# Chunked gated linear attention into a squared-ReLU FFN: all weight sums on VectorE, weight conversions closer together, attention pairs of the second group further apart

## The chip, the core and the metric

The kernel runs on one core of one Trainium2 chip. The metric is the device time of one execution in microseconds. Engines: TensorE (PE, with its weight loads PEld), VectorE (DVE), ScalarE (ACT), GpSimd (POOL), and SyncE (SP), whose queue issues all DMAs.

## What is computed

A gated linear recurrence over 768 tokens for 4 batches and 8 heads of width 48, and then a two-layer feed-forward network with squared ReLU over all 3072 tokens (model width 384, inner width 2048):

```python
for t in range(S):
    state = alpha[:, :, t, :, None] * state + np.einsum('bhd,bhe->bhde', k[:, :, t], v[:, :, t])
    y[:, :, t] = np.einsum('bhd,bhde->bhe', q[:, :, t], state)
...
h = np.maximum(x @ w_in, 0.0)
return (h * h @ w_out).astype(np.float32)
```

x is y with the heads side by side. The two weight matrices arrive as 64-bit floats; everything else is 32-bit.

## The kernel before

**Blocks and groups.** The tokens are cut into chunks of 128. Block n is chunk n//4 of batch n%4; there are 24 blocks. Four blocks (one chunk of every batch, 512 tokens) form a group; there are six. While the FFN of group g runs on TensorE, the attention of group g+1 is woven into it, in pairs of blocks.

**Attention of one block.** `ln` (logarithm of alpha, ACT), `cs` (cumulative sum as a product with a triangle, PE), `eb` and `ei` (exponentials, ACT), `mq` and `mk` (q and k scaled, L290, DVE), `turn` (transposes, L539, PE; PSUM tiles T), `kc` and `qc` (copies ks and qs, ACT). Then `ga` and `gb`: scores (L428) and sums for the state (L454) on PE, the mask `am` (L438) and the state's updates `us` and `s` (L465, L473, L474) on DVE, the products of y (L404) on PE, and `ev` (L562), which copies y into x on ACT. `ga` of a pair computes the scores of its first block and the first part of y of the pair before; `gb` does the scores of the second block and the rest of y.

The PSUM tiles of attention come in turn from one pool of four banks, `ps_att`: two for the transposes of each block, two for the scores of each block, two for the y of each pair, one for each `cs`. A tile can be written once the readers of the tile four places back are done. In the first group the scores of block 5 so take a bank that the scores of block 4 had (one `cs` lies between), and the scores of block 7 both banks of block 6 (with two of y between). The FFN has four banks of its own, `ps_ffn`.

**Conversion of the weights.** Each matrix comes in eight parts: w_in0 to 7 and w_out0 to 7, here also counted as index 0 to 15, 768 KB each in 64 bits, into four raw buffers. DVE takes exponent and upper mantissa out of the high words (L150, L154: `convert_first`), ACT turns the exponent and the low words (L163, L166: `convert_middle`), DVE puts them together (L172, L176, L179: `convert_second`). Indices 0 to 2 are started in a list written out by hand (`first`); the rest is spread over the first group by `next_weights`.

**FFN.** The first group multiplies plainly: units `ffn_in` j = 2 to 15 (L730, cost 2 each, 28 in all, with Relu and Square on ACT) and then 32 units `ffn_out` (L749, cost 1; part i of w_out is first used at unit 28 + 4i). The groups from the second on save products. The first layer (`layer_in`, L681, the order in the string `LAYER`) uses 20 sums of blocks of w_in (`W_SUMS`, `sum_w_in`) and 11 sums of blocks of x (`X_SUMS`, `sum_x`), all at L623. The second layer (`ffn_product`, L787) computes seven products for each four pairs of blocks in 28 units and needs sums of w_out: t1, t2, t3 (in place in w_out) and t4 for each of four r, 16 in all (`sum_w_out`). These sums are made once, the last ones during the second group.

**Who sets the order.** The program is recorded in one order, and each engine runs its instructions in that order. `weave` puts events between units: an event whose time is at most the sum of the costs so far is recorded ahead of the next unit. `attention` spreads the steps of a pair by the table `PLAN` (or `EARLY` in the first group), scaled: 2.35 in the first group, 1 later.

```python
events = [(4.0 * i, next_weights, ()) for i in range(2 * NW)]
```

At event i of these, load of index 4 + i, second half of index 2 + i, first half and middle of index 3 + i are recorded together.

Of the kernel before, what the change touches and what calls it, by code (L numbers as in the profile page):

```python
# [13 lines left out]
ALU = mybir.AluOpType  # L14
# [11 lines left out]
def kernel(  # L26
# [25 lines left out]
    nc = tc.nc  # L52
# [35 lines left out]
    NW = 8  # L88
# [3 lines left out]
    HM, NR2 = DM // 2, NJ // 4  # L92
# [29 lines left out]
    def load_weights(i):  # L122
        dst = (w_in + w_out)[i]
        dt = moe_w_in.dtype
        raw = dst if dt == FP32 else raw_pool.tile(list(dst.shape), dt, tag="raw", name="raw")
        raws[i] = raw
        if i < NW:
            src = moe_w_in[:, i * DF // NW : (i + 1) * DF // NW]
            nc.sync.dma_start(out=raw, in_=src.rearrange("(k r) f -> r k f", r=128))
        else:  # L130
            i -= NW
            src = moe_w_out[i * DF // NW : (i + 1) * DF // NW, :]
            nc.sync.dma_start(out=raw, in_=src.rearrange("(j r) m -> r j m", r=128))
# [6 lines left out]
    def convert_first(i):  # L140
        if moe_w_in.dtype == FP32:
            return
        w = (w_in + w_out)[i].rearrange("a k f -> a (k f)")
        n = w.shape[1]
        words = raws.pop(i).rearrange("a k f -> a (k f)").bitcast(U32)
        words = words.rearrange("a (n h) -> a n h", h=2)
        lo, hi = words[:, :, 0], words[:, :, 1]
        power = cv_pool.tile([128, n], U32, tag="power", name="power")
        upper = cv_pool.tile([128, n], U32, tag="upper", name="upper")
        nc.vector.tensor_scalar(  # L150
            out=power, in0=hi, scalar1=20, scalar2=0x7FF,
            op0=ALU.logical_shift_right, op1=ALU.bitwise_and,
        )
        nc.vector.tensor_scalar(  # L154
            out=upper, in0=hi, scalar1=0xFFFFF, scalar2=None, op0=ALU.bitwise_and
        )
        half[i] = w, lo, hi, power, upper

    def convert_middle(i):
        if moe_w_in.dtype == FP32:  # L160
            return
        w, lo, hi, power, upper = half[i]
        nc.scalar.activation(  # L163
            out=power, in_=power, func=AF.Relu, scale=2.0**23, bias=rebias
        )
        nc.scalar.activation(out=w, in_=lo, func=AF.Copy, scale=2.0**-52, bias=1.0)  # L166

    def convert_second(i):
        if moe_w_in.dtype == FP32:
            return  # L170
        w, lo, hi, power, upper = half.pop(i)
        nc.vector.scalar_tensor_tensor(  # L172
            out=power, in0=hi, scalar=0x80000000, in1=power,
            op0=ALU.bitwise_and, op1=ALU.bitwise_or,
        )
        nc.vector.scalar_tensor_tensor(  # L176
            out=w, in0=upper, scalar=2.0**-20, in1=w, op0=ALU.mult, op1=ALU.add
        )
        nc.vector.tensor_tensor(out=w, in0=w, in1=power.bitcast(FP32), op=ALU.mult)  # L179
# [1 line left out]
    for n, xs in ((0, "aqk"), (1, "aqk")):  # L181
        load(n, xs)
    to_load = list(range(2 * NW))
    stage = [3]

    def next_weights():
        i = stage[0]
        stage[0] += 1
        if to_load:
            load_weights(to_load.pop(0))  # L190
        if i <= 2 * NW:
            convert_second(i - 1)
        if i < 2 * NW:
            convert_first(i)
            convert_middle(i)


    NAM = 2
    am_t = kept("am", NAM, [128, 2, NP, 128])
# [418 lines left out]

    acc, ws, sums = {}, {}, {}

    def combine(steps, engine=nc.vector):
        for o, x, op, z in steps:
            engine.tensor_tensor(out=o, in0=x, in1=z, op=op)  # L623

    def parsed(text):
        for word in text.split():
            o, x, op, z = re.fullmatch(r"(\d+)=(\d+)([+-])(\d+)", word).groups()
            yield int(o), int(x), ALU.add if op == "+" else ALU.subtract, int(z)

    def w_slot(i):  # L630
        if i < 4 * KM:
            c, kk = divmod(i, KM)
            return w_in_t[:, 2 * c : 2 * c + 2, kk, :]
        r, i = divmod(i - 4 * KM, 3)
        if r not in ws:
            ws[r] = raw_pool.tile([128, 3, 2, 256], FP32, tag="raw", name="ws")
            if r == 2:
                sums.update({3: ws[r][:, 2]})
        return ws[r][:, i]
# [4 lines left out]

    w_sums = list(parsed(W_SUMS))

    def sum_w_in(i, engine):
        o, x, op, z = w_sums[i]
        combine(((w_slot(o), w_slot(x), op, w_slot(z)),), engine)

    def sum_x(g):
        if not xs_ready:
# [59 lines left out]
    def sum_w_out(i):  # L712
        i, r = divmod(i, NR2)
        t1, t2, t4 = (t[r] for t in tsum)
        b11, b12 = w_out[r][:, :, 0:HM], w_out[r][:, :, HM:DM]
        b21, b22 = w_out[NR2 + r][:, :, 0:HM], w_out[NR2 + r][:, :, HM:DM]
        o, x, z = ((t1, b12, b11), (t2, b22, t1), (b12, b22, b12), (t4, b21, t2))[i]
        combine(((o, x, ALU.subtract, z),), nc.gpsimd if i > 1 else nc.vector)

    def halves(j):  # L720
        return hid[j][:, :, 0:HT], hid[j][:, :, HT : 2 * HT]
# [49 lines left out]
    def ffn_product(g, i, r):  # L771
# [62 lines left out]
    steps = {f.__name__: f for stage in stages for f in stage}  # L834
# [12 lines left out]
        weights1 y0 cs3 ev0 br1 kT2 qT2 zeros2 ei3 kc2 qc2 kv1 eb3 mk3 load4v kT3 first0  # L847
        st0 mq3 weights2 load4q load4k middle0 sc2 kc3 qT3 second0 qc3 bl3 am2 br3 st1 br2
        kv2 sc3 am3 ha0 first1 ha1 middle1 y2 ev2 load4a hb0 first2 hb1 second1 st2 kv3
        middle2 st3 weights3  # L850
    """
    for word in first.split():
        f = max((x for x in steps if word.startswith(x)), key=len)
# [28 lines left out]
    def attention(pairs, scale):  # L882


        out = []
        for t, n0, after, *last in pairs:
            for at, fs in EARLY if n0 < SPLIT else PLAN:
                for f in fs.split():
                    w = t + at * scale
                    if f in ("ga", "gb"):  # L890
                        given = n0 - 2 if after else None, None if last or n0 >= NBLK else n0
                        out.append((w, {"ga": ga, "gb": gb}[f], given))
                    if last:
                        continue
                    if f == "ga" and n0 + 3 < NBLK:
                        out.append((w, load, (n0 + 3, "k")))
                    elif f == "gb":
                        for m, x in ((n0 + 2, "v"), (n0 + 3, "v"), (n0 + 4, "k")):
                            if m < NBLK:
                                out.append((w, load, (m, x)))  # L900
                    elif f == "turn":
                        if n0 < NBLK:
                            out.append((w, turn, (n0,)))
                            for m in range(n0 + 2, min(n0 + 4, NBLK)):
                                out.append((w, load, (m, "q")))
                    elif f != "ga" and n0 < NBLK:
                        n = n0 + int(f[-1])
                        out.append((w, steps[f[:-1]], (n,)))
                        if f[:-1] == "cs" and n + 2 < NBLK:
                            out.append((w, load, (n + 2, "a")))  # L910
        return sorted(out, key=lambda x: x[0])
# [13 lines left out]
    NG, NU = NBLK // GB, len(PRODUCTS) * NR2  # L925
    units = [(2, ffn_in, (0, j)) for j in range(2, NJ)]

    units += [(1, ffn_out, (0, t, i)) for i in range(NW) for t in range(GB)]
    events = [(4.0 * i, next_weights, ()) for i in range(2 * NW)]
    events += [(0, load, (GB + 1,)), (1.0, load, (GB + 2, "k"))]  # L930
    for i in range(len(w_sums)):
        at, engine = (44.1 + 0.5 * i, nc.gpsimd) if i < 9 else (51 + 0.2 * (i - 9), nc.vector)
        if i in (15, 16, 19):
            at, engine = 53.2, nc.gpsimd
        events.append((at, sum_w_in, (i, engine)))
    events += attention([(0, GB, False), (18.0, GB + 2, True), (27.5, GB + 4, True, True)], 2.35)
    events += [(54, sum_x, (1,))]
    weave(units, sorted(events, key=lambda x: x[0]))
    for g in range(1, NG):

        between = {}
        if g == 1:
            between = {3 + 5 * i: lambda i=i: sum_w_out(i) for i in range(4 * NR2)}
        layer_in(g, between)
        events = []
        if g + 1 < NG:
            n = GB * (g + 1) + 2
            pairs = [(0, n, True), (11.5, n + 2, True)]
            if g == 1:
                pairs = [(0, n - 2, False), (6.25, n, True), (12.5, n + 2, True)]  # L950
            events = attention(pairs, 1) + [(NU - 4.5, sum_x, (g + 1,))]
        weave([(1, ffn_product, (g, *u)) for u in PARTS], events)


# [28 lines left out]
```

## Time and profile before

| | us |
|---|---|
| median of three executions | 556.38 |
| lowest, highest | 553.46, 556.99 |
| profiled execution | 553.33 |
| span of its profile | 551.4 |

The page of the profile cuts the span into 40 slices of 13.8 us. A digit is the busy share in tenths; PEclk is the clock that TensorE was granted.

```profile
PE   8889999989999999999999999999999999999996
...
DVE  4988779599887773777673677664478651577530
ACT  4568875424264444236542327442326340326100
POOL 2010000562400000000000000000000000000000
PEclk9999999989999999999999999999999999999999
```

TensorE is the busy engine, except in the first three slices, in the ninth (110 to 124 us) and at the end. The first group lasts to 135.5 us, where L681 begins. GpSimd works in slices eight to twelve: these are the sums that the change moves. The costliest groups of instructions of those that the change concerns (busy in total, mean ns of one, then idle time of the engine ahead of them and what ended it):

```profile
L623 DVE TENSOR_TENSOR hid<-hid,h 128x512 f32<-128x512 f32 x130 | 88.4, 686 | 40.0 <-PE h L681 36.6
...
L749 PE MATMUL o<-w_out,hid 128*128 128x384 f32 x128 | 44.9, 505 | 2.9 <-DVE w_out L179 2.9
L730 PE MATMUL h<-x,w_in 128*128 128x512 f32 (+1 forms) x108 | 43.5, 551 | 3.3 <-ACT x L562 1.8
```

### The profile page before, as it was taken

How to read it: one execution, taken by the hardware profiler on the slowest of the kernel's cores; microseconds unless marked ns; L12 is line 12 of the kernel's file. 1: busy time of each engine (PE TensorE's matmuls, PEld its weight loads, DVE VectorE, ACT ScalarE, POOL GpSimd, SP SyncE). 2: the span in 40 equal slices, each digit the busy share in tenths (PEclk: the TensorE clock that was granted, in tenths of full speed). 3: DMA queues.
4: the chain of work that ended last, by engine and by line, in shares of the span. 5: the costliest groups of instructions: out<-in, count | busy, mean ns of one | idle time of the engine just before them, and what ended most of it. 6: DMA issues, size and time to landing. Idle time of an engine off the chain costs nothing.

```text
span 551.4 us, 12336 instructions
## 1 busy us (share of the span) xinstructions
PE 535.6 (97%) x5226; PEld 456.1 (83%) x5226; DVE 366.2 (66%) x636; ACT 236.0 (43%) x503; POOL 32.8 (6%) x46
## 2 busy tenths in 40 slices
PE   8889999989999999999999999999999999999996
PEld 5754456645889988988999988999988999988996
DVE  4988779599887773777673677664478651577530
ACT  4568875424264444236542327442326340326100
POOL 2010000562400000000000000000000000000000
PEclk9999999989999999999999999999999999999999
DMA  9977667511001654300342300153300000100001
GB/s 161 252 184 195 170 160 208 131 49 57 2 1 30 117 94 77 95 1 0 59 89 46 101 0 1 38 95 60 87 1 0 1 3 2 57 1 0 1 1 57
DMA packets 117086, 37.03 MB, mean 67 GB/s; under 512 B 108820, under 2 KB 111912, under 8 KB 117032
## 3 DMA queue, kind: packets, MB, share of 16 engines
q1 hardware_dynamic: 117032, 36.25, 28.9%
q8 instruction: 41, 0.67, 0.5%
q14 instruction: 13, 0.11, 0.1%
HBM read 31.49 MB, written 4.75 MB: 66 GB/s over the span
## 4 chain that ended last, share of the span: by engine, by line
PE 61%; DVE 2%; ACT 1%; issue 0%
PE o L787 29%; PE h L681 25%; PE y L404 3%; PE T L539 1%; PE sckv L428 1%; PE sckv L454 1%; ACT x L562 1%; PE cs L275 0%; DVE hid L623 0%; DVE am L438 0%; PE cs L274 0%; DVE us L812 0%; DVE hi L262 0%; DVE lo L263 0%; DVE s L473 0%
## 5 line engine op out<-in xcount | busy, mean ns | idle before, releaser
L623 DVE TENSOR_TENSOR hid<-hid,h 128x512 f32<-128x512 f32 x130 | 88.4, 686 | 40.0 <-PE h L681 36.6
L787 PE MATMUL o<-w_out,hid 128*128 128x192 f32 x480 | 82.6, 328 | 0.0
L787 PEld LDWEIGHTS o<-w_out,hid 128*128 128x128 f32 x480 | 78.5, 190 | 0.7
L681 PE MATMUL h<-xs,w_in 128*128 128x256 f32 x320 | 74.8, 379 | 0.0
L562 ACT COPY x<-y 32x256 f32<-32x256 f32 (+2 forms) x132 | 46.2, 364 | 55.5 <-PE y L404 52.1
L681 PEld LDWEIGHTS h<-xs,w_in 128*128 128x128 f32 x320 | 60.8, 190 | 8.1
L438 DVE COPY_PREDICATED am<-halves_mask,sckv 128x256 f32<-128x256 uint32 x40 | 15.6, 442 | 53.7 <-PE sckv L454 53.7
L681 PE MATMUL h<-x,ws 128*128 128x256 f32 x200 | 49.7, 380 | 0.0
L749 PE MATMUL o<-w_out,hid 128*128 128x384 f32 x128 | 44.9, 505 | 2.9 <-DVE w_out L179 2.9
L730 PE MATMUL h<-x,w_in 128*128 128x512 f32 (+1 forms) x108 | 43.5, 551 | 3.3 <-ACT x L562 1.8
L705 ACT COPY hid<-h 128x512 f32<-128x512 f32 x20 | 11.7, 585 | 78.0 <-PE h L681 78.0
L787 PE MATMUL o<-t,s 128*128 128x192 f32 x240 | 43.4, 328 | 0.0
L681 PEld LDWEIGHTS h<-x,ws 128*128 128x128 f32 x200 | 38.1, 190 | 5.1
L749 PEld LDWEIGHTS o<-w_out,hid 128*128 128x128 f32 x128 | 24.6, 197 | 20.5 <-DVE w_out L179 4.1
L681 PE MATMUL h<-x,w_in 128*128 128x256 f32 x160 | 40.3, 379 | 0.0
L787 PEld LDWEIGHTS o<-t,s 128*128 128x128 f32 x240 | 39.5, 190 | 0.3
L730 PEld LDWEIGHTS h<-x,w_in 128*128 128x128 f32 x108 | 20.1, 190 | 23.4 <-issue 16.2
L698 ACT ACTIVATE hid<-hid 128x512 f32<-128x512 f32 x55 | 34.7, 631 | 1.7
L681 PEld LDWEIGHTS h<-x,w_in 128*128 128x128 f32 x160 | 30.5, 190 | 4.1
L681 PE MATMUL h<-xs,ws 128*128 128x256 f32 x120 | 30.0, 380 | 0.0
L701 ACT ACTIVATE hid<-hid 128x512 f32<-128x512 f32 x35 | 22.0, 627 | 17.0 <-DVE hid L623 16.7
L787 PE MATMUL o<-t,hid 128*128 128x192 f32 x160 | 29.0, 332 | 0.0
(132 smaller groups left out, 786.8 us busy)
## 6 DMA issues: line engine op xcount, KB each, us to landing
raw<-in_moe_w_in_dram SPq DMA_DIRECT2D x8, 768.0 KB
raw<-in_moe_w_out_dram SPq DMA_DIRECT2D x8, 768.0 KB, 5.2
v_in<-in_v_dram SPq DMA_DIRECT2D x24, 192.0 KB, 4.4
out_dram<-osb SPq DMA_DIRECT2D x24, 192.0 KB, 2.0
k_in<-in_k_dram SPq DMA_DIRECT2D x23, 192.0 KB, 3.5
a_in<-in_alpha_dram SPq DMA_DIRECT2D x22, 192.0 KB, 2.6
q_in<-in_q_dram SPq DMA_DIRECT2D x22, 192.0 KB, 3.1
last<-row SPq DMA_DIRECT2D x40, 0.8 KB, 2.9
```

Of the source, the lines that this page charges most:

```text
L404: ins = nc.tensor.matmul(out=ys[e][64 * half : 64 * half + D + G * e, m % 2, p // 2, t], lhsT=lhsT, rhs=rhs, start=(half, e) not in seen, ...
L428: nc.tensor.matmul(out=ps[e][HALF[h], 0, p, :], lhsT=ks[rows, p, HALF[h]], rhs=qs[rows, p, HALF[h]], start=True, stop=True, skip_group_che ...
L438: nc.vector.copy_predicated(out=am_h(n)[:, e, n % 2], data=ps[e][:, 0], mask=halves_mask.bitcast(U32).unsqueeze(1).to_broadcast([128, NP, ...
L562: copy(out=x[to : to + m, kk, t : t + 2], in_=blk[n]["y"][e][r : r + m, :, p // 2],)
L623: engine.tensor_tensor(out=o, in0=x, in1=z, op=op)
L681: nc.tensor.matmul(out=banks[b][:, i, :], lhsT=w_slot(int(w))[:, "uv".index(p), i * 128 : (i + 1) * 128], rhs=x_slot(int(x)), start=(start ...
L698: nc.scalar.activation(out=t, in_=t, func=AF.Square)
L701: nc.scalar.activation(out=part(o), in_=operand(x), func=AF.Relu, scale=1.0 if sign == "+" else -1.0)
L705: nc.scalar.copy(out=part(word[0:2]), in_=operand(word[3:5]))
L730: nc.tensor.matmul(out=ps, lhsT=w[:, kk, c0 : c0 + 128], rhs=xT[g][:, kk, cols], start=(kk == 0), stop=(kk == KM - 1),)
L749: nc.tensor.matmul(out=acc[t][:, 0:DM], lhsT=hid[i][:, j, t * C : (t + 1) * C], rhs=w_out[i][:, j, :], start=(i == 0 and j == 0), stop=(i ...
L787: nc.tensor.matmul(out=acc[k][:, t, :], lhsT=lhs[:, j, t * C : (t + 1) * C], rhs=rhs[:, j, :], start=(first and r == R[0] and j + t == 0), ...
```

## The change

It takes the sums of weights away from GpSimd, gives all of them to VectorE one by one, and moves other events so that VectorE has room for them:

- The 20 sums of w_in: 12 were on GpSimd (nine from unit 44.1 in steps of 0.5, three at 53.2) and 8 on VectorE from unit 51 in steps of 0.2. Now all are on VectorE, one per unit of the first group's second layer from unit 36.
- The 16 sums of w_out: 8 on VectorE and 8 (t3 and t4) on GpSimd, all spread over the 2nd group's first layer every 5 words. Now VectorE does all: t1 and t2 every 10 words, t3 and t4 one per unit of the second layer.
- Conversions: first half and middle every 3.4 units instead of 4; the second half 1.5 units after the first instead of at the next event. One more load is recorded ahead (`weights4`), so that loads run two indices ahead of the conversion.
- In the second group the second and third pair start at 6.8 and 13.4 instead of 6.25 and 12.5. `sum_x` is recorded 11.5 after the start of the last pair: 24.9 instead of 23.5 in the second group, 23.0 instead of 23.5 in the later ones; in the first group at 55 instead of 54.

Nothing that is computed changes. In the order of instructions TensorE's is the same until the product stage of the second group.

```diff
-    stage = [3]
-
-    def next_weights():
-        i = stage[0]
-        stage[0] += 1
+
+    def next_weights(i):
         if to_load:
             load_weights(to_load.pop(0))
-        if i <= 2 * NW:
-            convert_second(i - 1)
-        if i < 2 * NW:
-            convert_first(i)
-            convert_middle(i)
+        convert_first(i)
+        convert_middle(i)
...
-        combine(((o, x, ALU.subtract, z),), nc.gpsimd if i > 1 else nc.vector)
+        combine(((o, x, ALU.subtract, z),))
...
-        middle2 st3 weights3
+        middle2 st3 weights3 weights4
...
-    events = [(4.0 * i, next_weights, ()) for i in range(2 * NW)]
+    events = [(3.4 * i, next_weights, (3 + i,)) for i in range(2 * NW - 3)]
+    events += [(3.4 * i + 1.5, convert_second, (3 + i,)) for i in range(-1, 2 * NW - 3)]
     events += [(0, load, (GB + 1,)), (1.0, load, (GB + 2, "k"))]
-    for i in range(len(w_sums)):
-        at, engine = (44.1 + 0.5 * i, nc.gpsimd) if i < 9 else (51 + 0.2 * (i - 9), nc.vector)
-        if i in (15, 16, 19):
-            at, engine = 53.2, nc.gpsimd
-        events.append((at, sum_w_in, (i, engine)))
+    events += [(36 + i, sum_w_in, (i,)) for i in range(len(w_sums))]
     events += attention([(0, GB, False), (18.0, GB + 2, True), (27.5, GB + 4, True, True)], 2.35)
-    events += [(54, sum_x, (1,))]
+    events += [(55, sum_x, (1,))]
...
-            between = {3 + 5 * i: lambda i=i: sum_w_out(i) for i in range(4 * NR2)}
+            between = {3 + 10 * i: lambda i=i: sum_w_out(i) for i in range(2 * NR2)}
...
-                pairs = [(0, n - 2, False), (6.25, n, True), (12.5, n + 2, True)]
-            events = attention(pairs, 1) + [(NU - 4.5, sum_x, (g + 1,))]
+                pairs = [(0, n - 2, False), (6.8, n, True), (13.4, n + 2, True)]
+            events = attention(pairs, 1) + [(pairs[-1][0] + 11.5, sum_x, (g + 1,))]
+        if g == 1:
+            late = [(0.5 + i, sum_w_out, (2 * NR2 + i,)) for i in range(2 * NR2)]
+            events = sorted(events + late, key=lambda x: x[0])
```

More of the change, by code (lines that the diff above doesn't have):

```diff
@@ L619, with combine @@
     acc, ws, sums = {}, {}, {}
-    def combine(steps, engine=nc.vector):
+    def combine(steps):
         for o, x, op, z in steps:
-            engine.tensor_tensor(out=o, in0=x, in1=z, op=op)
+            nc.vector.tensor_tensor(out=o, in0=x, in1=z, op=op)
     def parsed(text):
@@ L645, with sum_w_in @@
     w_sums = list(parsed(W_SUMS))
-    def sum_w_in(i, engine):
+    def sum_w_in(i):
         o, x, op, z = w_sums[i]
-        combine(((w_slot(o), w_slot(x), op, w_slot(z)),), engine)
+        combine(((w_slot(o), w_slot(x), op, w_slot(z)),))
     def sum_x(g):
```

## The prediction, made before the result was known

> **What bounds the kernel now.** I read the engine totals, then who TensorE waited for, then the timelines where it waited.
>
> ```profile
> PE 535.6 (97%) x5226; PEld 456.1 (83%) x5226; DVE 366.2 (66%) x636; ACT 236.0 (43%) x503; POOL 32.8 (6%) x46
> ```
>
> TensorE (PE) is busy for 97% of the span, so only its 15.8 us of gaps, and slow matmuls, can be won back. The waits of PE, in us in total, times, longest:
>
> ```profile
> PE o L749 <- DVE w_out L179: 2.9, 2, 2.3
> PE T L539 <- DVE q_in L290: 1.0, 1, 1.0
> PE T L539 <- ACT x L562: 0.5, 1, 0.5
> ```
>
> The other gaps lie in the first 39 us and the tail, where nothing is changed. The largest wait is for a converted block of second-layer weights on VectorE (DVE). Windows of 2 us around it (PE, PEld, DVE, ACT, POOL busy, then granted clock, DMA share, GB/s):
>
> ```profile
> 112.00:114.00 2.00, 0.67 (x3) 0.05 (x1) 1.97 (x2) 0.00 (x0) 1.92 (x2) 1.00 0.03 12
> 114.00:116.00 2.00, 0.99 (x2) 0.69 (x3) 2.00 (x2) 0.00 (x0) 1.92 (x2) 0.68 0.00 0
> 116.00:118.00 2.00, 2.00 (x5) 1.09 (x4) 1.47 (x3) 1.47 (x2) 0.08 (x1) 0.50 0.00 0
> ```
>
> PE stops and its clock falls to 0.50 afterwards. The PE and DVE timelines (start, duration) show the size and the cause:
>
> ```profile
> 105.95 6.72 PE L749 MATMUL o<-w_out,hid 128*128 128x384 f32 x20
> 115.01 4.38 PE L749 MATMUL o<-w_out,hid 128*128 128x384 f32 x8 [2.34 <-DVE w_out L179]
> 130.28 5.43 PE L749 MATMUL o<-w_out,hid 128*128 128x384 f32 x16 [0.57 <-DVE w_out L179]
> ```
> ```profile
> 94.87 0.96 DVE L172 SCALAR_TENSOR_TENSOR power<-raw,power 128x768 uint32<-128x768 uint32 x1 [0.54 <-ACT power L163]
> 106.09 0.78 DVE L438 COPY_PREDICATED am<-halves_mask,sckv 128x256 f32<-128x256 uint32 x2 [3.64 <-PE sckv L454]
> 109.06 2.02 DVE L172 SCALAR_TENSOR_TENSOR power<-raw,power 128x768 uint32<-128x768 uint32 x1
> 111.00 2.02 DVE L176 SCALAR_TENSOR_TENSOR w_out<-upper,w_out 128x768 f32<-128x768 uint32 x1
> 113.06 1.90 DVE L179 TENSOR_TENSOR w_out<-w_out,power 128x768 f32<-128x768 f32 x1
> ```
> ```profile
> 106.23 1.27 POOL L623 TENSOR_TENSOR w_in<-ws,w_in 128x512 f32<-128x512 f32 x1
> 110.34 1.86 POOL L623 TENSOR_TENSOR w_in<-w_in 128x512 f32<-128x512 f32 x1
> ```
>
> The second half of the conversion of w_out5 stood in DVE's queue behind two masks that waited for PE's scores, and then ran at half speed beside the sums on GpSimd (POOL). From 105.95 to 135.54, the start of the second group, pass 29.59 us. Its 68 matmuls of L749 at 0.33 us (28 take 9.23 us from 89.87) need 22.4, the products of y between them 2.2: the loss is **5.0 us**, of which 2.9 idle and 2.1 slow clock.
>
> **What the Trainium skill says.** "SBUF — State Buffer", section "Who interferes with whom": a DVE instruction with two SBUF inputs contends with a GpSimd instruction that reads SBUF. The trace agrees: L172 takes 0.95 alone and 2.02 beside GpSimd, a sum 1.27 becomes 1.86. "TensorE: Matmul & The Clock Gate", section "What's actually happening": the clock falls to half after an idle window of about 3.4 us. Here 2.34 us of idling sufficed, followed by clock 0.50; the measurement decides. "GPSIMD Engine Reference", section "Engine selection": two-input elementwise work is about 2x slower on GpSimd; here 1.27 against 0.69, 1.8x.
>
> **The change, part by part.** I laid out DVE's and ScalarE's (ACT) new queue order with the durations of the rows, start to start: a conversion on DVE is 0.47 + 0.47 (first half), 0.87 + 0.99 + 0.88 (second half), a scaling of k or q 0.47, a mask set with its state 1.95, a sum of w_in 0.68, of w_out 0.47 to 0.55; on ACT a conversion 1.63, Relu with Square 1.15, exponentials 0.37 each, four pairs of copies of k and q 2.1.
>
> *Sums to DVE, first group.* Twelve sums move: 12 x 0.69 = 8.3 us more for DVE. It gets back what GpSimd cost it between 107.67 and 127.4: 1.06 (L474), 1.07, 1.07, 0.94 (L172, L176, L179), 1.07 (L150), 1.07, 0.95, 1.07 (sums), together 8.3. So the load is even; what matters is the order.
>
> *Conversions every 3.4 units.* DVE's own cadence is the limit at first: until 51.3 us the order is the same. Then, in trace time:
> - q of block 5 is scaled after the conversion of w_in6 and not before w_in5: ready at 61.1, where PE transposes it at 61.11. Cost about 0.1 us.
> - w_out0 waits for ACT, which does copies from 65.6 to 67.7; ACT converts until 68.6, DVE's second half of w_out0 takes 2.74 to 71.4, the first half of w_out1 0.95, ACT is then late again (72.4 to 73.3), and the second half of w_out1 ends at 76.1. Only then comes the mask of block 4, at 76.1 instead of 73.24. The scores of block 5 (PE at 76.5) reuse a PSUM bank that this mask and L465 free at 77.2: **a new wait of 0.7**.
> - The mask of block 5 follows a first half and ends at 80.95 (79.0 + 1.95). From there DVE has no gap over 0.6: second half of w_out2 (83.7), a k, first half of 3, q, k, second half of w_out3 (88.8), q, w_out4 (93.5: 0.95, 0.54 of waiting for ACT, 2.74), w_out5 (97.7), two sums (99.1), w_out6 with one sum inside it (103.4), two sums: 104.8. So the mask of block 6 starts at 104.8, not 100.38. The scores of block 7 (PE at 105.7) need its banks, free at 106.4: **a new wait of 0.7**.
> - PE asks for w_out5 at about 114 and for w_out7 (ready at 111.7) at 127. Both old waits and the slow clock go: **minus 5.0**.
> - The weights are loaded two conversions ahead instead of one; DVE's 2.8 us wait at 68.3 for a load goes, hidden either way.
> - Thirteen sums remain after the mask of block 7 (113.7): done by 122.5. The sums of x wait for ACT's last copies (127.4); the one that PE needs first is ready at 129.1, PE arrives at 132.1. Cost nothing.
>
> These two waits are the least certain terms. The cost from below is 0 (DVE 0.7 us earlier each time), from above about 2 each, if every handover from ACT to DVE costs 0.1 us more than in the rows (some 20 of them before block 6). I take 0.7 each.
>
> *Second group.* Eight sums of w_out move from GpSimd into DVE's queue in the product stage: 8 x 0.47 = 3.8 us, against gaps of DVE of 0.19, 1.31, 0.97, 0.59 and 2.51 from 174 to 187, together 5.6. By the layout the scaled q for the transposes is ready 9.5 us after the stage begins and PE takes it at 10.7; the corrections of s come 0.1 to 0.8 later, with PE units of 1.3 us between them and their use. Hidden, cost nothing.
>
> *Pairs further apart.* The transposes come one unit (1.3 us) later on PE while DVE reaches q at the same 24.5 us into the stage: the wait of 1.0 goes. The wait of 0.5 for ACT stays, because copies and transposes move together. The sums of x have one unit less before the next group, with 0.8 us to spare by the layout: cost 0 to 0.5, I take 0.1. In later groups only an output sum goes behind the sums of x; its bank is asked for about 4 us into the layer. Nothing.
>
> Sum: -5.0 + 0.1 + 0.7 + 0.7 - 1.0 + 0.1 = **-4.4 us**, some 547 for the span of the profile.
>
> From which time? The runs of before are 553.46, 556.38 and 556.99, the profiled one 553.33. From the median I get 552.0, from the profiled run 548.9. A fall of the clock has no fixed phase against the program (the same page of the skill calls the window free-running; no run here shows it), and contention an order that can vary; I expect part of the scatter to go with both. I take the middle, **550.6**.
>
> **The rivals.**
> - *Complete gain.* DVE is a little earlier than laid out, no new wait, and the scatter goes. -6.0 from 553.4: 547.4. For it: each new wait is only 0.7. Against it: DVE has no gap from 81 to 105.
> - *The wait moves.* The masks, now behind conversions and sums, hold PE for 2 us each time and q of block 5 for 1: -5.0 + 5.0 - 1.0 = -1.0, about 555.4. For it: DVE follows its queue strictly, and sums that are not urgent stand ahead of a mask that frees banks.
> - *Slower.* As before, but a wait of 2.3 or more at block 7 drops the clock again (2.1), DVE's backlog delays the second group by 2, and the transposes there still wait (1.0): -1.0 + 2.1 + 2.0 + 1.0 = +4.1, about 560.5. Against it: DVE has over 4 us to recover after block 7.
>
> **How the numbers follow.** Forecast 0.5, complete gain 0.15, the wait moves 0.27, slower 0.08. The range reaches from just under the complete gain, 546.8, to the moved wait, 556.0. One per cent is 550.8: the complete gain and about half the forecast, which straddles it, lie below, plus a little for scatter: faster 0.44, same 0.49, slower 0.07.
>
> **What would show it.** After: no wait of L749 on the conversion, clock near 1 throughout 112 to 120, GpSimd idle there, L172 at 0.95; short waits of PE before the scores of blocks 5 and 7 on DVE; no wait of the transposes on q in the second group; the second group begins near 132. I am wrong if the scores wait for over 1.5 us, if layer L681 of the second group waits, or if the old wait was not what slowed the clock.

## The result, and the profile after

The changed kernel takes 549.12 us (median; 548.91 to 549.96), the kernel before beside it 554.95 us (553.46 to 556.99): a ratio of 0.9895, with a 95% interval of 0.9853 to 0.9937. The time is in the predicted range, 1.5 us under the forecast of 550.6. The span of the profiled execution went from 551.4 to 547.4 us, 4.0 less, where 4.4 less was forecast. The medians lie further apart, by 5.8: the profiled execution of before (553.33) was one of its faster ones. Lines of the changed code have numbers that are 7 lower than before in this part: L742 is `ffn_out`, L674 `layer_in`, L780 `ffn_product`, L421 the scores, L431 the mask, L458 `us`, L532 the transposes, L616 every sum.

The engine totals of the changed kernel:

```profile
PE 534.2 (98%) x5226; PEld 455.3 (83%) x5226; DVE 368.6 (67%) x656; ACT 235.8 (43%) x503; POOL 5.9 (1%) x26
```

PE's gaps are 13.2 us now (15.8 before), and GpSimd has 5.9 us of work left, all in the first 33 us. The waits of PE (us in total, times, longest):

```profile
PE sckv L421 <- DVE us L458: 1.0, 1, 1.0
PE qT L308 <- DVE w_out L283: 0.9, 1, 0.9
```

The wait of 2.9 us of `ffn_out` on the conversions is gone, and in this profile so are both waits of the transposes in the second group. One wait is new: scores on `us`. The windows at the place where PE had stopped (PE, PEld, DVE, ACT, POOL busy, granted clock, DMA share, GB/s):

```profile
112.00:114.00 2.00, 2.00 (x7) 1.17 (x7) 1.93 (x5) 1.92 (x6) 0.00 (x0) 1.00 0.00 0
114.00:116.00 2.00, 2.00 (x7) 1.14 (x6) 1.96 (x4) 0.15 (x1) 0.00 (x0) 1.00 0.01 4
116.00:118.00 2.00, 2.00 (x44) 1.16 (x46) 1.97 (x4) 0.00 (x0) 0.00 (x0) 1.00 0.00 0
```

PE is full, its clock 1.00, GpSimd idle. The price stands a little earlier, in PE's timeline (start, duration, the wait ahead in brackets):

```profile
104.99 0.69 PE L397 MATMUL y<-am,v_in 64*48 64x64 f32 x32
106.66 1.07 PE L421 MATMUL sckv<-qs,ks 48*64 48x64 f32 x29 [0.98 <-DVE us L458]
...
108.18 9.30 PE L742 MATMUL o<-w_out,hid 128*128 128x384 f32 x28
...
132.80 2.54 PE L674 MATMUL h<-xs,w_in 128*128 128x256 f32 x11
```

These are the scores of block 7. Where nothing holds them, as in the kernel before, they begin 0.48 us after the products of y ahead of them (104.39 to 104.87), and `ffn_out` 1.08 after that. Here PE could have begun them at 105.47, and `ffn_out` begins at 108.18, which is 2.71: the handover costs 1.63. The trace counts only 0.98 of it as idling, since the products of y are still draining at first, and the scores, once begun, are held a second time by the later reader of their other bank (L466, which reads until 107.04). From 108.18 to the second group at 132.80 pass 24.62 us: 68 matmuls at 0.33 (22.4) and two pieces of y (2.2), with no loss. DVE's timeline shows what stood ahead of the mask of block 6, whose `us` frees the bank:

```profile
98.48 0.69 DVE L616 TENSOR_TENSOR ws<-w_in 128x512 f32<-128x512 f32 x1
...
104.11 0.69 DVE L616 TENSOR_TENSOR w_in<-ws,w_in 128x512 f32<-128x512 f32 x1
104.83 0.69 DVE L616 TENSOR_TENSOR ws<-w_in 128x512 f32<-128x512 f32 x1
105.44 0.77 DVE L431 COPY_PREDICATED am<-halves_mask,sckv 128x256 f32<-128x256 uint32 x2
106.10 0.42 DVE L458 TENSOR_TENSOR us<-sckv,s 128x256 f32<-128x256 f32 x1
...
109.69 0.95 DVE L172 SCALAR_TENSOR_TENSOR power<-raw,power 128x768 uint32<-128x768 uint32 x1
```

PE had finished the mask's input at 100.9; the mask began at 105.44, behind the second half of w_out6 and the sums around it. L172 takes 0.95 us here, at 109.69; at 109.06 before it took 2.02.

Where the time went, by the starts of the stages in us:

| | `ffn_out` | second group | third group | end of span |
|---|---|---|---|---|
| before | 80.88 | 135.54 | 226.87 | 551.4 |
| after | 81.49 | 132.80 | 222.80 | 547.4 |
| difference of the stage up to there | +0.61 | -3.35 | -1.33 | +0.1 |

The whole gain lies in the second half of the first group and in the second group. The -3.35 is the old loss of 5.0 less the new 1.63; the +0.61 is 0.23 at the transposes of block 5 and some 0.4 of waiting at start-up (`qT`, 0.9 instead of 0.4), which moved between 0.3 and 1.6 from profile to profile.

### The profile page after: what moved, and what is told of

It reads as the page before. It is cut to its first block, busy times and chain, and to the rows that moved or that the text cites. A ratio compares the mean times of both kernels' runs of the same rounds, so it can differ in the third digit from the quotient of the medians.

```text
span 547.4 us, 12320 instructions
## 1 busy us (share of the span) xinstructions
PE 534.2 (98%) x5226; PEld 455.3 (83%) x5226; DVE 368.6 (67%) x656; ACT 235.8 (43%) x503; POOL 5.9 (1%) x26
## 3 DMA queue, kind: packets, MB, share of 16 engines
HBM read 31.49 MB, written 4.75 MB: 66 GB/s over the span
## 4 chain that ended last, share of the span: by engine, by line
PE 81%; DVE 10%; ACT 4%; issue 2%; DMA 2%; SPq 0%; POOL 0%; DVEq 0%; POOLq 0%
PE o L780 33%; PE h L674 32%; PE o L742 4%; PE y L397 4%; PE sckv L421 2%; PE T L532 2%; PE sckv L447 2%; ACT power L163 1%; DMA raw<-in_moe_w_in_dram 1%; DVE w_out L176 1%; DMA raw<-in_moe_w_out_dram 1%; DVE power L172 1%; DVE power L150 1%; DVE w_in L176 1%; DVE w_out L179 1%
## 5 line engine op out<-in xcount | busy, mean ns | idle before, releaser
L616 DVE TENSOR_TENSOR hid<-hid,h 128x512 f32<-128x512 f32 x130 | 88.4, 687 | 40.5 <-PE h L674 37.0
L780 PE MATMUL o<-w_out,hid 128*128 128x192 f32 x480 | 82.3, 327 | 0.0
L780 PEld LDWEIGHTS o<-w_out,hid 128*128 128x128 f32 x480 | 78.5, 190 | 0.6
L674 PE MATMUL h<-xs,w_in 128*128 128x256 f32 x320 | 74.8, 379 | 0.0
L674 PEld LDWEIGHTS h<-xs,w_in 128*128 128x128 f32 x320 | 60.7, 190 | 8.3
L674 PE MATMUL h<-x,ws 128*128 128x256 f32 x200 | 49.7, 379 | 0.0
L431 DVE COPY_PREDICATED am<-halves_mask,sckv 128x256 f32<-128x256 uint32 x40 | 15.5, 441 | 43.7 <-PE sckv L447 43.7
L780 PE MATMUL o<-t,s 128*128 128x192 f32 x240 | 43.2, 328 | 0.0
L742 PE MATMUL o<-w_out,hid 128*128 128x384 f32 x128 | 42.8, 490 | 0.0
L674 PEld LDWEIGHTS h<-x,ws 128*128 128x128 f32 x200 | 38.0, 190 | 5.2
L674 PE MATMUL h<-x,w_in 128*128 128x256 f32 x160 | 40.2, 379 | 0.0
L780 PEld LDWEIGHTS o<-t,s 128*128 128x128 f32 x240 | 39.5, 190 | 0.3
L742 PEld LDWEIGHTS o<-w_out,hid 128*128 128x128 f32 x128 | 23.9, 190 | 16.2 <-issue 0.5
L674 PEld LDWEIGHTS h<-x,w_in 128*128 128x128 f32 x160 | 30.4, 190 | 4.1
L674 PE MATMUL h<-xs,ws 128*128 128x256 f32 x120 | 30.0, 379 | 0.0
L780 PE MATMUL o<-t,hid 128*128 128x192 f32 x160 | 28.8, 331 | 0.0
```

The costliest lines, as they stand in the source:

```text
L431: nc.vector.copy_predicated(out=am_h(n)[:, e, n % 2], data=ps[e][:, 0], mask=halves_mask.bitcast(U32).unsqueeze(1).to_broadcast([128, NP, ...
L616: nc.vector.tensor_tensor(out=o, in0=x, in1=z, op=op)
L674: nc.tensor.matmul(out=banks[b][:, i, :], lhsT=w_slot(int(w))[:, "uv".index(p), i * 128 : (i + 1) * 128], rhs=x_slot(int(x)), start=(start ...
L742: nc.tensor.matmul(out=acc[t][:, 0:DM], lhsT=hid[i][:, j, t * C : (t + 1) * C], rhs=w_out[i][:, j, :], start=(i == 0 and j == 0), stop=(i ...
L780: nc.tensor.matmul(out=acc[k][:, t, :], lhsT=lhs[:, j, t * C : (t + 1) * C], rhs=rhs[:, j, :], start=(first and r == R[0] and j + t == 0), ...
```

## The experiments

The theory: the old wait needed two conditions together, the **order** (the second half of w_out5 behind masks that wait for PE) and the **contention** (the sums on GpSimd that lengthen DVE's rows). The rivals: one of the two alone carries it. A second question is what the new wait at block 7 comes from, a third why the clock fell. "1st" below is the time from the first `ffn_out` to the second group, "2nd" the length of the second group. Each ratio is to the kernel before on the same chip.

| run | median us | ratio, 95% | span | 1st | 2nd |
|---|---|---|---|---|---|
| before (median beside after; profile shown above) | 554.95 | | 551.4 | 54.66 | 91.33 |
| after | 549.12 | 0.9895 [0.9853, 0.9937] | 547.4 | 51.31 | 90.00 |
| e1 conversions alone | 551.38 | 0.9925 [0.9896, 0.9954] | 550.9 | 49.68 | 91.89 |
| e2 sums alone | 550.09 | 0.9900 [0.9879, 0.9921] | 548.0 | 49.72 | 91.24 |
| e3 pairs alone | 554.95 | 0.9983 [0.9970, 0.9997] | 553.5 | 56.46 | 90.22 |
| e4 before without GpSimd's sums | 550.50 | 0.9909 [0.9885, 0.9933] | 549.1 | 49.98 | 92.40 |
| e5 e4 with DVE work as delay | 554.99 | 0.9987 [0.9971, 1.0003] | 552.7 | 53.62 | 92.18 |
| e6 after, sums later | 547.96 | 0.9860 [0.9835, 0.9886] | 545.8 | 49.68 | 90.01 |
| e7 after, conversions as before | 548.21 | 0.9864 [0.9840, 0.9887] | 545.3 | 49.68 | 89.63 |
| e8 after, late w_out sums on GpSimd | 550.12 | 0.9896 [0.9875, 0.9917] | 547.1 | 51.26 | 89.56 |
| e9 after again | 549.55 | 0.9893 [0.9875, 0.9911] | 547.8 | 51.30 | 89.97 |
| e10 e6 again | 547.68 | 0.9858 [0.9837, 0.9879] | 545.8 | 49.67 | 90.06 |
| e11 e7 again | 548.51 | 0.9872 [0.9850, 0.9894] | 547.0 | 50.25 | 89.57 |

### Each part of the change alone

**Conversions alone (e1).** The sums stay on GpSimd, the pairs where they were.

```diff
-    events = [(4.0 * i, next_weights, ()) for i in range(2 * NW)]
+    events = [(3.4 * i, next_weights, (3 + i,)) for i in range(2 * NW - 3)]
+    events += [(3.4 * i + 1.5, convert_second, (3 + i,)) for i in range(-1, 2 * NW - 3)]
```

> Before with the conversions every 3.4 units alone; all sums stay where they were, on GpSimd and VectorE; pairs as before. My theory: the old wait needs two things at once, a second half of w_out5 queued behind the masks of blocks 6 and 7, and GpSimd reading beside it. This run takes away the first alone: w_out5 is ready near 98 to 100 us, no wait of L749 on the conversion, the clock stays at 1.00, 5.0 us come back less what GpSimd's contention does to the masks (up to 2.5 us at the scores of block 7): span 546.5 to 549, time about 549 to 551. Rival, contention alone: the slowed conversions make PE wait as before (2 us or more of L749 on DVE), span 550 or more.

The first group loses nothing after `ffn_out` begins (49.68), though GpSimd sums from 105.3 to 125 and DVE's rows beside it are as slow as ever. DVE's timeline of e1:

```profile
104.54 0.96 DVE L179 TENSOR_TENSOR w_out<-w_out,power 128x768 f32<-128x768 f32 x1
105.42 0.77 DVE L432 COPY_PREDICATED am<-halves_mask,sckv 128x256 f32<-128x256 uint32 x2
...
111.27 2.02 DVE L172 SCALAR_TENSOR_TENSOR power<-raw,power 128x768 uint32<-128x768 uint32 x1
```

Contention is there (2.02) and harmless: w_out5 and w_out6 were ready by 105.5. "Contention alone" falls. Nor do the scores of block 7 wait: the mask of block 6, at 105.42, stands ahead of the slow rows. The span is nevertheless only 0.5 less, because in this execution the start went badly. The windows of e1:

```profile
22.00:24.00 2.00, 0.49 (x10) 0.30 (x6) 1.94 (x6) 1.66 (x3) 0.00 (x0) 1.00 0.78 205
24.00:26.00 2.00, 1.93 (x16) 1.79 (x18) 1.97 (x4) 1.12 (x3) 0.00 (x0) 0.85 1.02 274
26.00:28.00 2.00, 2.00 (x17) 1.78 (x16) 1.97 (x3) 0.00 (x0) 0.00 (x0) 0.50 0.96 337
```

A wait of 1.6 at 22 to 24 us (`qT`), with GpSimd idle, is followed by clock 0.50 until 32 us, and `ffn_out` begins 3.3 us late. Of the four executions of e1 two had a mean clock of 1.00, and took 549.69 and 551.42; the median, 551.38, is just above the 549 to 551 that were expected.

**Sums alone (e2).** All sums on DVE at the times of the change; conversions every 4.0, pairs as before.

```diff
-        at, engine = (44.1 + 0.5 * i, nc.gpsimd) if i < 9 else (51 + 0.2 * (i - 9), nc.vector)
...
+    events += [(36 + i, sum_w_in, (i,)) for i in range(len(w_sums))]
...
-        combine(((o, x, ALU.subtract, z),), nc.gpsimd if i > 1 else nc.vector)
+        combine(((o, x, ALU.subtract, z),))
```

> Before with all sums of weights on VectorE, placed as in the changed kernel; conversions every 4 units and pairs as before. It takes away GpSimd's contention alone and leaves the second half of w_out5 behind the masks. Theory: from the rows, w_out5 ready at 111.5 (PE asks at 112.7), w_out7 at 124.4 (asked at 125.3), block 6's mask at 101.4 (banks asked at 104.9): no wait in the first group, -5.0, so a span of about 546.5 with the second group's transposes still waiting about 1.0; time about 548.5. Rival, order alone: the wait for w_out5 stays, made longer by sums ahead of it in the queue: span 550 or more.

No wait of `ffn_out`, and none of the scores either. DVE's timeline of e2:

```profile
101.72 0.77 DVE L437 COPY_PREDICATED am<-halves_mask,sckv 128x256 f32<-128x256 uint32 x2
...
106.69 0.78 DVE L437 COPY_PREDICATED am<-halves_mask,sckv 128x256 f32<-128x256 uint32 x2 [1.57 <-PE sckv L453]
...
109.21 0.95 DVE L172 SCALAR_TENSOR_TENSOR power<-raw,power 128x768 uint32<-128x768 uint32 x1
```

The second half of w_out5 still stands behind the masks and begins at 109.21, as before (109.06). It takes 0.95 + 0.95 + 0.96 and not twice that, ends at 112, and PE asks at about 113. "Order alone" falls. With e1 this shows that either edit removes the old wait, so their gains do not add. The span, 548.0, is 1.5 above what was expected: 0.56 had been lost by the start of `ffn_out` (81.44), and from the third group on e2 takes 325.6 against 324.5. That last part lies between 324.5 and 325.9 in all the profiles; its cause is not known.

**Pairs alone (e3).**

```diff
-                pairs = [(0, n - 2, False), (6.25, n, True), (12.5, n + 2, True)]
-            events = attention(pairs, 1) + [(NU - 4.5, sum_x, (g + 1,))]
+                pairs = [(0, n - 2, False), (6.8, n, True), (13.4, n + 2, True)]
+            events = attention(pairs, 1) + [(pairs[-1][0] + 11.5, sum_x, (g + 1,))]
```

> Before with the second group's pairs further apart alone (6.8, 13.4, and the sums of x at 11.5 after the last pair). Theory: the wait of the transposes on q (1.0) goes, the first group keeps its waits and its slow clock: span 551.4 - 1.3 = 550.1, and single executions still scatter by about 3 us. Rival: the pairs do nothing, because the last wait only moves to the next transposes: span 551.4.

The second group is 1.11 us shorter (90.22), as expected, and the wait on q is gone. The span is not: it is 2.1 longer than in the profile of before. The first group, which this edit does not touch, lost more. PE's timeline of e3, and the windows after its two waits:

```profile
115.18 2.85 PE L749 MATMUL o<-w_out,hid 128*128 128x384 f32 x8 [2.34 <-DVE w_out L179]
...
130.57 6.80 PE L749 MATMUL o<-w_out,hid 128*128 128x384 f32 x15 [2.22 <-DVE w_out L179]
```
```profile
114.00:116.00 2.00, 0.82 (x3) 0.55 (x4) 2.00 (x2) 0.00 (x0) 1.92 (x2) 1.00 0.00 0
...
130.00:132.00 2.00, 1.43 (x4) 0.87 (x5) 1.93 (x4) 0.00 (x0) 0.00 (x0) 0.84 0.00 0
132.00:134.00 2.00, 2.00 (x5) 1.09 (x4) 1.83 (x5) 0.49 (x1) 0.00 (x0) 0.50 0.00 0
```

The first wait is the same 2.34 as before, but the clock stayed at 1.00 after it. PE so came to w_out7 1.36 us earlier, at 128.35 (130.57 less the wait) instead of 129.71, and gained nothing, since w_out7 was not ready sooner. GpSimd's last three sums, which wait for PE's products of y, began at 119.79 instead of 121.15 and lay over the first half of w_out7, on DVE, and less over the sums behind it. DVE's timeline of e3, and the last of the rows in that of before:

```profile
120.41 1.62 DVE L150 TENSOR_SCALAR power<-raw 128x768 uint32<-128x768 uint32 x1
121.95 1.63 DVE L154 TENSOR_SCALAR upper<-raw 128x768 uint32<-128x768 uint32 x1
...
129.56 0.96 DVE L179 TENSOR_TENSOR w_out<-w_out,power 128x768 f32<-128x768 f32 x1
```
```profile
129.26 0.96 DVE L179 TENSOR_TENSOR w_out<-w_out,power 128x768 f32<-128x768 f32 x1
```

In the profile of before L150 and L154 take 0.55 each here, and the sums behind them longer; w_out7 is done 0.30 later in e3. So the second wait became 2.22 instead of 0.57, 1.36 of the difference because PE came earlier and the rest because DVE was later. This time the clock fell after the wait, and the 16 matmuls up to the second group took 6.96 (130.57 to 137.53) instead of 5.26. The slow clock after the first wait, in the profile of before, had therefore cost next to nothing of its own: PE that is not slowed there waits for w_out7 instead. The old loss thus differs from execution to execution, and over twelve of e3 the pairs' part shows as -0.17%, an interval that barely leaves out no change.

### The old wait, taken apart

**Without GpSimd's sums (e4).** The twelve sums of w_in on GpSimd are left out: six become a memset of their slot (the slot is filled with zeros) and six are dropped, so the first layer of the later groups computes with wrong sums. All else is as before.

```diff
+    def clear_slot(i, engine):
+        if w_sums[i][0] >= 4 * KM:
+            engine.memset(w_slot(w_sums[i][0]), 0.0)
...
-        events.append((at, sum_w_in, (i, engine)))
+        events.append((at, sum_w_in if engine is nc.vector else clear_slot, (i, engine)))
```

> Before, but the 12 sums of w_in on GpSimd are left out: those into new slots become memsets of the slot (6 on GpSimd, which read nothing), those in place are dropped, so the output is not the reference's. VectorE's order is untouched. Theory, contention: VectorE's rows between 107 and 127 fall from about 2.0 to 0.95 us, w_out5 is ready at 110.8, before PE asks at 112.7; no wait, clock 1.00, span 546.4, time about 548.5, and the scatter of 3 us between executions goes. Rival, order alone: PE waits over 1 us for w_out5 all the same, span 549 or more.

DVE's timeline of e4:

```profile
108.42 0.42 DVE L474 TENSOR_TENSOR s<-s,last 128x256 f32<-128x256 f32 x1
108.77 0.95 DVE L172 SCALAR_TENSOR_TENSOR power<-raw,power 128x768 uint32<-128x768 uint32 x1
```

The queue is that of the kernel before, the rows are short again, and the wait and the slow clock are gone: the second group begins 49.98 after the first `ffn_out`, 4.7 sooner than before. The span was a miss, 549.1 instead of 546.4: the second group took 92.4, with a stop of PE of 0.73 at the products of y that the trace puts down to "issue" (no wait that the profile shows) and that nothing here explains, and the profiled execution was the longest of four (the spans of the others are 547.2 to 548.7).

**The stop of PE without GpSimd's sums (e5).** e4, with a memset and six additions on DVE ahead of the second half of w_out5, on a spare tile. It leaves out the same sums.

```diff
+        if i - 1 == NW + 5:
+            idle = xs_t[:, 8:10].rearrange("a i t -> a (i t)")
+            nc.vector.memset(idle, 0.0)
+            for _ in range(6):
+                nc.vector.tensor_tensor(out=idle, in0=idle, in1=idle, op=ALU.add)
```

> e4 (GpSimd's sums of w_in left out, so the output is not the reference's) plus one memset and six additions of 128x512 on VectorE ahead of the second half of w_out5, 4.1 us by the rows (0.3 + 6 x 0.63). GpSimd reads nothing here. Theory: w_out5 is ready at about 115, PE waits about 2.2 us for it as before, and the granted clock of the executions falls from about 1.00 (e4) to 0.997 or less (before), since the idling of PE is enough for a fall: span 549.1 + 2.2 + up to 1.7 = 551 to 553. Rival: the fall of the clock belongs to GpSimd's work beside PE: clock stays at 1.00, span 551.3 at most.

PE's timeline of e5, and the windows after the wait:

```profile
117.59 2.85 PE L758 MATMUL o<-w_out,hid 128*128 128x384 f32 x8 [3.10 <-DVE w_out L179]
```
```profile
116.00:118.00 2.00, 0.41 (x1) 0.30 (x2) 1.97 (x4) 0.00 (x0) 0.30 (x1) 1.00 0.00 0
118.00:120.00 2.00, 2.00 (x8) 1.14 (x6) 1.47 (x4) 1.74 (x2) 0.00 (x0) 1.00 0.00 0
```

3.10 us of idling, where 2.2 were expected (the memset and the additions took 4.75 and not 4.1), and in this execution no fall of the clock. In twenty executions the mean granted clock went from 0.992 to 1.000. The ten at 0.997 or more took 552.31 to 554.91 (mean 553.5), the ten at 0.996 or less 555.06 to 557.63 (mean 556.0). Where in those ten the clock was low their records do not say, but e4, which differs only by the delay, had one clock of 0.996 and three of 1.000. The ten with a high clock take 3.2 us more than those three of e4 (mean 550.3), about the stop itself. So low clocks and a scatter like that of the kernel before come without GpSimd's sums of w_in, with a stop of PE, in some executions and not in others, and go with about 2.5 us more. (GpSimd's eight sums of w_out are left in, but begin only at 136 us.) That they come from the stop rests on the comparison with e4's four executions, and is likely more than shown.

### The new wait at block 7

**Sums later (e6, and again e10).** In the changed kernel the 20 sums of w_in begin at 40.5 and follow every 0.7 units.

```diff
-    events += [(36 + i, sum_w_in, (i,)) for i in range(len(w_sums))]
+    events += [(40.5 + 0.7 * i, sum_w_in, (i,)) for i in range(len(w_sums))]
```

> The changed kernel with the 20 sums of w_in from unit 40.5 in steps of 0.7 instead of from 36 in steps of 1, so that none stands ahead of the mask of block 6. Theory: that mask starts 3.4 us earlier (near 102), the scores of block 7 find their banks free, the 1.6 us lost there come back; the second group begins at 131.2 instead of 132.8, span 545.8, time about 547.5. Rival: VectorE is the bound of this stretch and the wait only moves to w_out6, w_out7 or the sums of x: span 547 or more, with a wait of L749's or L681's kind.

DVE's timeline of e6:

```profile
101.84 0.96 DVE L179 TENSOR_TENSOR w_out<-w_out,power 128x768 f32<-128x768 f32 x1
102.72 0.77 DVE L431 COPY_PREDICATED am<-halves_mask,sckv 128x256 f32<-128x256 uint32 x2
...
104.70 0.68 DVE L616 TENSOR_TENSOR ws<-w_in 128x512 f32<-128x512 f32 x1
```

The mask of block 6 begins 2.72 us earlier, the sums follow it, and the scores of block 7 wait for nothing. The first group takes 49.68 from `ffn_out` on instead of 51.31: 1.63, the size of the wait.

**Conversions as before (e7, and again e11).** The changed kernel with conversions every 4.0 units, so sums and pairs of the change without its middle part.

```diff
-    events = [(3.4 * i, next_weights, (3 + i,)) for i in range(2 * NW - 3)]
-    events += [(3.4 * i + 1.5, convert_second, (3 + i,)) for i in range(-1, 2 * NW - 3)]
+    events = [(4.0 * i, next_weights, ()) for i in range(2 * NW)]
```

> The changed kernel with the conversions of before (every 4 units, one load less ahead). Theory: the closer conversions bring nothing once GpSimd is out of the way, and they are what puts sums and conversions ahead of block 6's mask: first group as in e2 (second group begins near 131.2), second group as in the changed kernel (90.0): span 545.8, 1.6 less than the changed kernel, time about 547.5. Rival: the margins of 1 us for w_out5 and w_out7 do not hold when loads jitter, and PE waits for a conversion again: span 547.4 or more.

No wait of `ffn_out`, none of the scores. So the closer conversions bring nothing once GpSimd is out of the way, and with them the sums stand early enough to hold up the mask: it takes both to make the new wait, and moving either removes it.

**Late sums of w_out back on GpSimd (e8).**

```diff
-        combine(((o, x, ALU.subtract, z),))
+        eng = nc.gpsimd if i > 1 else nc.vector
+        eng.tensor_tensor(out=o, in0=x, in1=z, op=ALU.subtract)
```

> The changed kernel with the eight late sums of w_out (t3, t4) back on GpSimd, at the changed kernel's places. Theory: on VectorE they are hidden, so nothing is gained: the second group takes 90.0 +- 0.5, span 547.4, and a few VectorE rows of the product stage double beside GpSimd. Rival: VectorE is short of time there (3.8 us of sums against 5.6 us of gaps): the second group gets at least 1 us shorter.

GpSimd made its eight sums from 132.7 to 161, in the first layer and not in the product stage: each began as soon as DVE had made the t1 or t2 that it needs. So they did not fall where they were meant to, and the slower rows that were expected did not appear. The second group takes 89.56, in after 90.00, and in e7, with all sums on DVE, 89.63. The eight sums on DVE thus cost between nothing and 0.4 us.

**The three versions side by side.** After, e6's kernel and e7's kernel once more, on one chip beside one another.

> The changed kernel itself, beside the two versions that follow, for a comparison on one chip. Expected as measured: 549.1 +- 0.7, about 0.989 to 0.990 of before.

> The version of e6 (sums of w_in from unit 40.5 in steps of 0.7) again, in five rounds. Theory: 1.6 us below the changed kernel of the same call, since the wait for the scores' banks is gone: about 547.5 to 548. Rival: the difference of the single profiles is within the scatter of executions: less than 0.5 us.

> The version of e7 (changed kernel with the conversions of before) again, in five rounds. Theory: equal to e6's version within 0.5 us and 1 to 1.6 us below the changed kernel. Rival: its margins of 1 us make it scatter more, and its median is not below the changed kernel's.

Medians are 549.55, 547.68 and 548.51. Every execution of e10 (547.26 to 548.28) lies below every one of e9 (549.35 to 550.43): later sums make the changed kernel 1.87 us faster, and beat both kernels. e11 (547.62 to 549.53) lies between, 0.83 above e10 where at most 0.5 was expected, and scatters more. No wait for a conversion shows in its profile; its first group is 0.57 longer than in e7, of which 0.30 is a stop at the products of y that the trace puts down to "issue".

## Why the prediction was right, step by step

The sum of the spans, term by term (forecast, then measured from the stages above):

| step | forecast | measured |
|---|---|---|
| old wait and slow clock at `ffn_out` | -5.0 | -5.0 |
| q of block 5 later | +0.1 | +0.23 |
| new wait at the scores of block 5 | +0.7 | 0 |
| new wait at the scores of block 7 | +0.7 | +1.63 |
| second group: transposes, sums of x | -0.9 | -1.33 |
| start-up, not in the forecast | 0 | +0.4 |
| later groups | 0 | +0.1 |
| sum | -4.4 | -4.0 |

**The old loss.** Right in cause and size. e2, with no wait in the first group, needs 49.72 from the first `ffn_out` to the second group, the kernel before 54.66: 4.94. The reason given, order and contention together, is shown by e1, e2 and e4, each of which removes one of them and with it the wait. The split into 2.9 of idling and 2.1 of slow clock is less good. The eight matmuls at half clock take 4.31 (115.01 to 119.32) instead of 2.64, 1.67 more; the rest of the 2.1 is spread in small pieces around the two waits. And e3 shows that the two parts are not separate gains: what the clock does not take, the wait for w_out7 takes.

**Scores of block 5: the step that failed.** It rested on the pool's four banks going round strictly in turn, so that these scores get a bank of block 4. In the profile of after they do not wait at all, though DVE was later than laid out. PE's and DVE's timelines:

```profile
77.07 0.69 PE L421 MATMUL sckv<-qs,ks 48*64 48x64 f32 x32
```
```profile
76.83 0.78 DVE L431 COPY_PREDICATED am<-halves_mask,sckv 128x256 f32<-128x256 uint32 x2
77.50 0.42 DVE L458 TENSOR_TENSOR us<-sckv,s 128x256 f32<-128x256 f32 x1
```

PE begins while block 4 is still being read. In the built program the scores of block 4 have banks 2 and 1, and for block 5 the pool hands out 3 and 0 (before: 3 and 2); bank 0 held a cumulative sum that ACT had read. With bank 2 PE would have had to wait until `us` ended at 77.92, some 0.85 by these rows, so the term was sized well and stood on the wrong bank. For block 7 the forecast's assignment holds in both kernels.

**Scores of block 7: right place, size 1.63 instead of 0.7.** The mask of block 6 came at 105.44, not 104.8, 0.64 later, and with it the last reader of its banks (L466 ended at 107.04, not 106.4). And PE was there at 105.47, not 105.7: it had not waited at block 5, which outweighs the 0.5 by which start-up and q had delayed it beyond the forecast. Both add to the 0.7: 1.57. The prediction had this end in its bounds ("about 2 each").

The two terms together are 1.4 forecast and 1.63 measured, and this is not two errors that happen to cancel. From the mask of block 5 to that of block 6 DVE's only gaps in the profile of after are two waits of 0.54 and 0.53 for ACT's part of a conversion, so the rows say that its mask of block 6 comes when it comes, however long PE is held at block 5. What PE does not wait there it waits here. The prediction did not say that its two terms hang together in this way, and no run held PE at block 5 to test it. The prediction had called a wait above 1.5 us at the scores a sign of its being wrong: the idling is 0.98, the whole delay 1.63, so counted as delay that sign has come. e6 and e7 show the cause as given: conversions and sums ahead of the mask.

**Pairs.** The wait on q went as forecast. The other wait, 0.5 for ACT, is not in the profile of after, but in e6, e7 and e8 it is (0.4 to 0.5), and also in e9, the same kernel, whose second group is no longer for it (89.97). So its absence does not explain that the second group gained 1.33 and not 0.9; what does is not shown.

**w_out sums on DVE.** Hidden, as forecast, within 0.4 (e8 against e7).

**The base.** From the profiled execution of before the working gave 548.9, from the median 552.0, and the middle was taken on the ground that part of the scatter would go. All of it that mattered went: the median of after is 549.12, its profiled execution 549.13, the executions lie within 1.05 us (before: 3.5). The ground agrees with e5, whose stop of PE brought the scatter back; "part" was too cautious by 1.5 us. The branch from the profiled execution, 548.9, would have met the time to 0.2, because that execution was one of the faster ones: 23 others of before on one chip lie between 553.64 and 557.47. The middle was a hedge between two bases and not a working.

**The rivals.** "The wait moves" was right in kind and wrong in size: one new wait of 1.63 came, not 5.0 us of waits. "Complete gain" is what e6 shows to be there to be had: 545.8 of span, 547.7 to 548.0 of time.

## What to carry to other kernels

A wait that needs two conditions together goes when either is removed, so two remedies for it do not add up, and the second can bring a wait of its own: price each alone and keep the one that puts nothing new in front of a waiting reader. Waits along one queue are not separate terms either: an engine that is let through at one place can meet the same late partner at the next (w_out7 in e3, block 7 here). On an engine that works strictly in order, work that is merely early, such as sums that nobody asks for yet, belongs behind the instruction that frees a bank, not ahead of it. Which bank a pool hands out is read from the built program, not assumed to go round in turn.

## What the runs showed of the hardware

- **The clock after a stop of PE.** The prediction took the fall after 2.34 us as given. It is not: 2.34 us was followed by 0.50 in the profile of before and by 1.00 in e3; 3.10 us by 1.00 in e5. The Trainium skill, "TensorE: Matmul & The Clock Gate", section "What's actually happening", calls the monitor's window of about 3.4 us free-running against the program. That equal stops have unequal outcomes agrees with it, but the phase itself is not in the records, so this cause is argued, not shown. The same may lie behind the low clock at the start of e1, after 1.6 us of waiting; what makes the wait there vary between 0.3 and 1.6 us stays open.
- **Contention adds much the same time to a DVE instruction whatever its length; it is not a factor.** The prediction reads L172 beside GpSimd as running "at half speed" (0.95 to 2.02). Other rows of before, on DVE undisturbed, then beside GpSimd, and GpSimd's own:

```profile
74.82 0.42 DVE L474 TENSOR_TENSOR s<-s,last 128x256 f32<-128x256 f32 x1
77.89 0.55 DVE L150 TENSOR_SCALAR power<-raw 128x768 uint32<-128x768 uint32 x1
```
```profile
107.67 1.48 DVE L474 TENSOR_TENSOR s<-s,last 128x256 f32<-128x256 f32 x1
114.88 1.62 DVE L150 TENSOR_SCALAR power<-raw 128x768 uint32<-128x768 uint32 x1
```
```profile
112.28 1.86 POOL L623 TENSOR_TENSOR ws<-w_in 128x512 f32<-128x512 f32 x1
```

L474, L150 and L172 are of three lengths, and each gets 1.06 to 1.07 us longer (L179 gets 0.94; a row at the edge of GpSimd's work can get less). DVE's rows (109.06 to 111.00) and GpSimd's (110.34 to 112.28) then follow one another at the same pace, 1.94. This agrees with the two engines taking turns by whole instructions, each waiting while the other runs. The Trainium skill, "SBUF — State Buffer", section "Who interferes with whom", says of DVE's two-port modes, which it allows for `tensor_scalar` (L150), that the engine that comes second blocks fully; whether L150 ran in such a mode no run shows. Rows with one input in PSUM were not slowed: L465 took 0.41 at 106.76, in the middle of a sum on GpSimd (106.23, 1.27 long).
